# A gated mix of a Fourier layer and a SwiGLU layer: one row's product moved into a matrix, and comparisons moved in a hand-written queue

## The chip, the cores and the metric

The kernel runs on one core of one Trainium2 chip. Its engines are TensorE (matmul; PE in the profile, PEld its weight loads), VectorE (DVE), ScalarE (ACT), GpSimd (POOL) and SyncE (SP, which here only issues transfers). Matrix products land in PSUM, eight banks of 2 KB per partition; everything else is in the 128-partition SBUF. The metric is the device time of one execution in microseconds.

## The reference

For x of 2048 x 512 in float32 the result is g * a + (1 - g) * b:

```python
g = sigmoid((x * gate_w).sum(-1, keepdims=True))
# a: real part of a DFT over both axes, by the matrices handed in
a = dft_seq_re @ (x @ dft_hid_re.T) - dft_seq_im @ (x @ dft_hid_im.T)
# b: SwiGLU, hidden width 1376
b = (silu(x @ w1) * (x @ w3)) @ w2
```

## The kernel before, in words

Every float32 product is done as three fp32r products of a high and a low part (`mm3`: high-high, high-low, low-high). So each operand is split: `high` is a copy by ScalarE, `low` a subtraction by VectorE. TensorE runs the whole time, in these stages:

1. **Start** (C): the first product of gate/up, while x and the first weights are still arriving. Eleven warm-up matmuls (`wps`) go ahead of it. x's first quarter matrix `B11` is one load of 512 KB by SP, behind the first quarter of the weights `ws0`.
2. **Gate/up**, items 1 to 21: `gate_up(n)` makes one tile of `h = silu(gate) * up` by a Strassen-like scheme of seven half-size products, in banks X, Y and Z. `ITEMS` lists (chunk of the hidden width, half of the rows). In each item the products come in a fixed order: X, Z, the first product of item n+3, X, Z, the second product of item n+3, X. VectorE adds them up (`u4`, line 353; `u2`, lines 361 and 362; the last product, line 377). `h` goes to memory (`store_h`, issued by POOL), and so do the split second weights `wb`.
3. **H**: `h @ w2`, 22 steps of 24 matmuls (11 chunks, twice: once for each half of the rows), each into eight banks in the order `HB`. Each step loads a tile of `h` four steps ahead and splits it two steps ahead (`load_h`, `high_h`, `low_h`; `load_w2`, `high_w2`, `low_w2`). For steps 0 and 1 the splits are in the last item of gate/up, at its `mid` place, that is ahead of that item's lines 361 and 362 on VectorE. At the end of each half ScalarE and VectorE evict the banks, scaled by 1 - g (`nb`).
4. **O1, O2, E2**: the DFT over the rows, from parts of x that were added up by symmetry beforehand (`XF`) times folded DFT matrices (`MV`). Results are split into `Z`. Single rows that the folding leaves over are multiplied as products with one contracted row (`edge_p`, `er_p`).
5. **Y**: the DFT over the columns, ten units. A unit has an even part and an odd part in one pair of PSUM banks. In the even part the row of column 128 is a product of its own with one contracted row (`dx_p`), three matmuls between the two others. VectorE then does `r = Y * g + nb` in four operations (two for the last four units, which have half the rows), and SP stores `r`.

The fast way is right only if the DFT matrices have the symmetries of a DFT. So the kernel also **compares**: for each of the folded matrices O2, O1a, O1b and E2 (16 tiles of 512 KB each) it loads 15 tiles, subtracts the first from each or adds it (`differ`, VectorE, lines 699 to 705), and sums absolute values (`add_up`, ScalarE, line 710). Seven smaller tiles (`dh`) and one of single values go the same way. `verdict` then turns the sums into a flag, `verdict_end` counts it by a matmul, and if anything deviates a general path runs at the end (`tc.If`); with these inputs it doesn't.

These comparisons and the work on x (`make_pair`, `odd_part`, `spread`, `high_x`, `low_x`; in places POOL adds single rows, from `lone` on) are **tasks in a queue** that is filled in at build time, in program order: O2's comparisons, the pair sums of x, the `dh` comparisons, the forms of x, then O1a, O1b and E2. At fixed places of gate/up, H, O1, O2 and Y a call `work(engine, us)` takes the first tasks of that engine that are ready until the budget `us` is spent: a task is taken while the budget is at least its cost less `over`. A task is ready if its load was issued `LAG` calls ago (2 in gate/up, 4 in H) and the task before it has been taken. After each call `load_ahead` issues the loads of the next tasks, as long as there is a place in `F4` (SBUF tiles of 4 KB per partition, shared with the loads of `h` and `w2`), a token (`RATE` of them per call), and fewer than `AHEAD` open tasks. `LIMIT` says how far into the queue gate/up may reach: `n_spare` up to item 11, `n_gate` after it. Until item 11 has ended, `F4` has four places; the gate/up budgets for VectorE are 2.4 us in items 9 to 12 and 4.2 us after that. SP works its loads off in program order, and each load waits until its place has been read for the last time.

Of the kernel before, what the change touches and what calls it, by code (L numbers as in the profile page):

```python
# [30 lines left out]
def fnet_swiglu_gate_kernel(  # L31
# [60 lines left out]
    HELD = {}  # L92
# [13 lines left out]
    def free(*tiles):  # L106
        for t in tiles:
            _, places, at = HELD.pop(id(t))
            places.append(at)
# [56 lines left out]
    def load_xo(g, k):  # L166
# [4 lines left out]
        nc.sync.dma_start(ST[g, k], xt[g, XRAW.index(k)])  # L171
# [20 lines left out]
    def load_w(w, lo=0, hi=4):  # L192
        if lo == 0:
            WS[w] = f4_a.tile([P, 4, 256], F32, tag=f"f4_{4 + w % (LOOK + 1)}", name=f"ws{w}")
        nc.sync.dma_start(WS[w][:, lo:hi].rearrange("p a n -> p (a n)"),
                          w13[SETS[w], :, lo * 256 : hi * 256])
# [186 lines left out]
    load_w(0, 0, 1)  # L383
    load_xo(0, "B11")
# [171 lines left out]
    COLD, LAND, TOKENS, RATE = [], [4], [1.0], [0.9]  # L556
# [11 lines left out]
    def load_ahead(n):  # L568
        thaw()
        for i in ORDER:  # L570
# [3 lines left out]
            if sum(k not in ISSUED for k in LOADED) >= n or len(F4) < need + temps + HELD_BACK[0] + RES[0]:  # L574
# [9 lines left out]
    def work(eng, us, most=9, lag=None, over=0.3):  # L584
# [5 lines left out]
        for i in ORDER[:LIMIT[0]]:  # L590
# [5 lines left out]
            if i not in LOADED or NOW[0] - LOADED[i] < lag:  # L596
# [11 lines left out]
    AHEAD = [26]  # L608
# [62 lines left out]
    def high_x(form):  # L671
        XF[form] = [take(F4, [P, 1024], F32R, f"xf{h}_{form}") for h in range(2)]
# [122 lines left out]

    def make_d():
        def highs():
# [3 lines left out]
            nc.scalar.activation(DT[:, 0, 258:516], d[:, 258:516], AF.Copy, scale=-1.0)  # L801

        def lows():
# [3 lines left out]
            nc.vector.tensor_sub(DT[:, 1, 258:516], DT[:, 0, 516:].bitcast(F32), d[:, 258:516])  # L807
            free(DH.pop(1))
# [52 lines left out]
    def high_edges():  # L861
        high(edge_p[:1, 0], edge[:1])
        high(er_p[:1, 0], rowm[:1, :258])
        high(dx_p[:1, 0], rowm[:1, 258:388])
        high(lone_p[:, 0], lone_a)

    def low_edges():
        low(edge_p[:1, 0], edge_p[:1, 1], edge[:1])
        low(er_p[:1, 0], er_p[:1, 1], rowm[:1, :258])
        low(dx_p[:1, 0], dx_p[:1, 1], rowm[:1, 258:388])  # L870
# [8 lines left out]
    def lone():  # L879
# [4 lines left out]
        r0, r1 = ROWS  # L884
        nc.sync.dma_start(r0[:1], edges[:, :1024])
# [29 lines left out]
        g.memset(edge[:1, 257:258], 0.0)  # L915
# [9 lines left out]
    n_spare = 17  # L925
# [19 lines left out]
    do(early, SPARE[0], nc.vector.memset, tail, 0.0)  # L945
    for n in range(SPARE[0], NI):
        do(early, n, work, "D", 2.4 if n < SPARE[1] else 4.2 if n < NI - 3 else 3.2 if n < NI - 1 else 1.0)
# [7 lines left out]
    HB = (2, 3, 4, 5, 7, 6, 0, 1)  # L955
# [541 lines left out]
```

## Time and profile before

| | |
|---|---|
| runs | 369.67, 369.93, 370.22 us; median 369.93 |
| profiled execution | 370.23 us, of which the span from first to last instruction is 368.4 us |
| granted TensorE clock, mean | 0.995 |
| TensorE, VectorE, ScalarE busy | 357.5, 313.6, 234.9 us |
| moved by transfers | 102.79 MB, mean 279 GB/s |
| stages by the chain of waits: start, gate/up, H, O1 to E2, Y | from 5.6, 16.7, 206.9, 322.8, 338.3 us |

In a row of the timeline the first number is the start in us from the span's start, the second the duration of the merged instructions (`x12` merges twelve), then engine, line, operation and output<-inputs with shapes; a bracket at the end gives the idle time before and what ended it. In a row of a table by stretch, each engine's busy time and number of instructions follow the stretch's length, in the order TensorE, its weight loads, VectorE, ScalarE, POOL; then granted clock, transfer share and GB/s.

### The profile page before, as it was taken

How to read it: one execution, taken by the hardware profiler on the slowest of the kernel's cores; microseconds unless marked ns; L12 is line 12 of the kernel's file. 1: busy time of each engine (PE TensorE's matmuls, PEld its weight loads, DVE VectorE, ACT ScalarE, POOL GpSimd, SP SyncE). 2: the span in 40 equal slices, each digit the busy share in tenths (PEclk: the TensorE clock that was granted, in tenths of full speed). 3: DMA queues.
4: the chain of work that ended last, by engine and by line, in shares of the span. 5: the costliest groups of instructions: out<-in, count | busy, mean ns of one | idle time of the engine just before them, and what ended most of it. 6: DMA issues, size and time to landing. Idle time of an engine off the chain costs nothing.

```text
span 368.4 us, 5140 instructions
## 1 busy us (share of the span) xinstructions
PE 357.5 (97%) x1750; PEld 309.8 (84%) x1750; DVE 313.6 (85%) x433; ACT 234.9 (64%) x394; POOL 56.3 (15%) x95
## 2 busy tenths in 40 slices
PE   9999999999999999999999799999999999999982
PEld 5888888888888888888888688888888888898871
DVE  4999989999678897887878899889999799848991
ACT  5875766656666786774433665585589899784810
POOL 0001222111111111111110593700110020000000
PEclk9999999999999999999999999999999999999998
DMA  7549866666327889999998299775599999970584
GB/s 287 225 173 333 341 233 243 247 240 252 109 75 241 274 290 390 386 391 330 411 404 245 100 311 408 266 284 181 179 342 413 409 408 409 410 286 0 177 282 175
DMA packets 31922, 102.79 MB, mean 279 GB/s; under 512 B 5650, under 2 KB 5907, under 8 KB 29844
## 3 DMA queue, kind: packets, MB, share of 16 engines
q1 hardware_dynamic: 27060, 81.96, 61.1%
q0 software_dynamic: 4832, 20.46, 14.3%
q8 instruction: 15, 0.25, 0.3%
q14 instruction: 15, 0.12, 0.1%
HBM read 77.76 MB, written 24.65 MB: 278 GB/s over the span
## 4 chain that ended last, share of the span: by engine, by line
PE 84%; DVE 10%; ACT 3%; issue 1%; DMA 0%; SPq 0%; DVEq 0%; ACTq 0%
PE H L126 29%; PE X L126 28%; PE Z L126 14%; PE Y L126 7%; PE C L126 3%; DVE r L1237 3%; DVE t L705 2%; PE wps L388 1%; ACT nb L1098 1%; DVE z_O L115 1%; DVE ht L115 1%; DVE w2t L115 1%; PE Y L1210 1%; ACT z_O L112 1%; ACT t L710 1%
## 5 line engine op out<-in xcount | busy, mean ns | idle before, releaser
L126 PE MATMUL H<-w2t,ht 128*128 128x512 f32 (+1 forms) x528 | 114.5, 379 | 1.8 <-DVE h L361 1.8
L126 PEld LDWEIGHTS H<-w2t,ht 128*128 128x128 f32 (+1 forms) x528 | 99.6, 189 | 16.5 <-DVE h L361 2.2
L126 PE MATMUL X<-xo,wb 128*128 128x512 f32 x378 | 88.6, 379 | 0.0
L126 PEld LDWEIGHTS X<-xo,wb 128*128 128x128 f32 x378 | 71.4, 189 | 10.1
L710 ACT ACTIVATE t<-t 128x1024 f32<-128x1024 f32 (+1 forms) x68 | 67.7, 997 | 13.6 <-DVE t L699 5.9
L302 POOL DMA_DIRECT2D hs<-h x36 | 19.5, 543 | 99.3 <-DVE h L362 70.5
L699 DVE TENSOR_TENSOR t<-t,rep 128x1024 f32<-128x1024 f32 x28 | 32.9, 1218 | 1.8 <-DMA t<-wt 1.8
L373 ACT ACTIVATE h<-X 128x512 f32<-128x512 f32 x21 | 12.5, 595 | 28.7 <-PE X L126 28.3
L126 PE MATMUL X<-xo,wa 128*128 128x512 f32 x126 | 30.6, 379 | 0.0
L126 PE MATMUL Y<-xo,wa 128*128 128x512 f32 x126 | 30.6, 379 | 0.0
L126 PE MATMUL Z<-xo,wb 128*128 128x512 f32 x126 | 30.6, 379 | 0.0
L126 PE MATMUL Z<-xo,wa 128*128 128x512 f32 x126 | 30.6, 379 | 0.0
L701 DVE TENSOR_TENSOR t<-t,rep 128x1024 f32<-128x1024 f32 x24 | 28.2, 1218 | 0.0
L126 PEld LDWEIGHTS X<-xo,wa 128*128 128x128 f32 x126 | 23.8, 189 | 3.4
L126 PEld LDWEIGHTS Y<-xo,wa 128*128 128x128 f32 x126 | 23.8, 189 | 3.4
L126 PEld LDWEIGHTS Z<-xo,wb 128*128 128x128 f32 x126 | 23.8, 189 | 3.4
L126 PEld LDWEIGHTS Z<-xo,wa 128*128 128x128 f32 x126 | 23.8, 189 | 3.4
L112 ACT ACTIVATE ht<-hr 128x1024 fp32r<-128x1024 f32 x19 | 20.0, 1052 | 8.3 <-issue 6.3
L353 DVE TENSOR_TENSOR u<-u,X 128x512 f32<-128x512 f32 x21 | 14.4, 687 | 12.7 <-PE X L126 9.0
L115 DVE TENSOR_TENSOR ht<-hr,ht 128x1024 fp32r<-128x1024 f32 x19 | 23.1, 1216 | 0.9 <-ACT ht L112 0.9
L115 DVE TENSOR_TENSOR wa<-ws,wa 128x768 fp32r<-128x768 f32 (+1 forms) x22 | 19.3, 880 | 5.1 <-ACT wa L112 4.9
L112 ACT ACTIVATE wa<-ws 128x768 fp32r<-128x768 f32 (+2 forms) x21 | 16.9, 807 | 9.8 <-DMA ws<-w 6.2
(201 smaller groups left out, 499.2 us busy)
## 6 DMA issues: line engine op xcount, KB each, us to landing
t<-wt SPq DMA_DIRECT2D x60, 512.0 KB, 9.3
hr<-hs SPq DMA_DIRECT2D x19, 512.0 KB, 7.7
hs<-h POOLq DMA_DIRECT2D x36, 256.0 KB, 4.2
wbsp<-wb POOLq DMA_DIRECT2D x8, 1024.0 KB, 4.3
wb<-wbsp SPq DMA_DIRECT2D x8, 1024.0 KB, 9.6
ws<-w SPq DMA_DIRECT2D x11, 512.0 KB, 4.9
xs_B<-xt SPq DMA_DIRECT2D x8, 512.0 KB, 5.3
xr<-xw SPq DMA_DIRECT2D x8, 512.0 KB, 9.6
```

What stands on the lines that cost most here:

```text
L112: nc.scalar.activation(hi, src, AF.Copy)
L115: nc.vector.tensor_sub(lo, src, hi.bitcast(F32))
L126: nc.tensor.matmul(ps.rearrange("p (n a) -> p n a", a=2), u, turns(v)[:, some], **kw)
L302: nc.gpsimd.dma_start(hs[c][:, b * TB : (b + 1) * TB], h)
L353: nc.vector.tensor_add(u4, u4, x)
L373: nc.scalar.activation(g1, x, AF.Silu)
L388: nc.tensor.matmul(wps, warm[:, :P], warm, start=True, stop=True)
L699: nc.vector.tensor_sub(t, t, r)
L701: nc.vector.tensor_add(t, t, r)
L705: nc.vector.tensor_tensor(tv, tv, r[:, None, 512 * im : 512 * im + 512].to_broadcast([P, 2, 512]), op=ALU.add if im else ALU.subtract)
L710: nc.scalar.activation(t[:, :n], t[:, :n], AF.Abs, accum_out=acc[:, i : i + 1])
L1237: nc.vector.scalar_tensor_tensor(rv[:, :, h], src, g_pos[:, k : k + 1], nv[:, :, h], op0=ALU.mult, op1=ALU.add)
```

## The change

- `dx`, the row of column 128, is written (high and low part) into row 0 of the first 130 columns of both imaginary parts in `DT`. That row was zero, as sin(0) is. The product with the imaginary part then contains it, and the separate product with `dx_p` goes.
- `edge` and `rowm` are zeroed by POOL on all partitions, and `edge_p` and `er_p` are split and multiplied with all 128 partitions instead of one.
- From the end of item 4 to the end of item 15 the two places `ZO` (free in that time) are lent to `F4`. `n_spare` goes from 17 to 32, which is all of O2's comparisons; VectorE's budgets in items 9 to 12 are 1.2, 4.6, 3.5 and 3.5 us; ScalarE gets a call in items 5 to 8.
- Queue: `AHEAD` 14, counting only tasks with loads; at most four places held back; `RATE` 0.75 in the second half of H; larger budgets and a lag of 2 in the last step of H; in Y smaller budgets, and the rest of the queue and `verdict` at unit 4 instead of 7.
- `low_h(1)` and `low_w2(1)` move to the end of the last item; bank 7 is last in `HB`; `next_two` takes the PSUM pairs in another order.
- x's first load is in two pieces; the first weights' load is issued by ScalarE's queue, and so are the stores of the last two units.

```diff
+            if places is not F4 or at not in GONE:
+                places.append(at)
...
-    def load_xo(g, k):
+    def load_xo(g, k, pieces=1):
...
+        n = 1024 // pieces
+        for i in range(pieces):
+            nc.sync.dma_start(ST[g, k][:, i * n : i * n + n], xt[g, XRAW.index(k), :, i * n : i * n + n])
...
-    load_w(0, 0, 1)
-    load_xo(0, "B11")
+    load_w(0, 0, 1, nc.scalar)
+    load_xo(0, "B11", 2)
...
-            if sum(k not in ISSUED for k in LOADED) >= n or len(F4) < need + temps + HELD_BACK[0] + RES[0]:
+            if sum(k not in ISSUED and QUEUE[k][5] > 0 for k in LOADED) >= n or len(F4) < need + temps + min(HELD_BACK[0], HOLD[0]) + RES[0]:
...
-            if i not in LOADED or NOW[0] - LOADED[i] < lag:
+            if i not in LOADED or NOW[0] - LOADED[i] < lag or temps and len(F4) < temps + RES[0]:
...
-    AHEAD = [26]
+    AHEAD = [14]
...
     def high_x(form):
+        F4.sort(key=lambda at: at[0] is f4_a)
...
+    def first_d(h):
+        return DT[:1, h, 258:].rearrange("p (b m) -> p b m", b=2)[:, :, :130]
+    def dx_row():
+        return rowm[:1, None, 258:388].to_broadcast([1, 2, 130])
...
+            high(first_d(0), dx_row())            # in make_d, highs
+            low(first_d(0), first_d(1), dx_row()) # in make_d, lows
...
-        high(edge_p[:1, 0], edge[:1])
-        high(er_p[:1, 0], rowm[:1, :258])
-        high(dx_p[:1, 0], rowm[:1, 258:388])
+        high(edge_p[:, 0], edge)
+        high(er_p[:, 0], rowm[:, :258])
...
+        g.memset(rowm, 0.0)
+        g.memset(edge, 0.0)
...
-        g.memset(edge[:1, 257:258], 0.0)
...
-    n_spare = 17
+    n_spare = 32
...
+    do(at_end, SPARE[0] - 5, lend)
+    do(at_end, SPARE[1] + 2, give_back)
+    for n in range(SPARE[0] - 4, SPARE[0]):
+        do(second, n, work, "A", 1.3)
...
-        do(early, n, work, "D", 2.4 if n < SPARE[1] else 4.2 if n < NI - 3 else 3.2 if n < NI - 1 else 1.0)
+        do(early, n, work, "D", (1.2, 4.6, 3.5, 3.5)[n - SPARE[0]] if n < SPARE[1] else
+           4.2 if n < NI - 3 else 3.2 if n < NI - 1 else 1.0)
...
-    HB = (2, 3, 4, 5, 7, 6, 0, 1)
+    HB = (2, 3, 4, 5, 6, 0, 1, 7)
...
-        do(mid, NI - 1, low_h, m)
-        do(mid, NI - 1, low_w2, m)
+        do(at_end if m else mid, NI - 1, low_h, m)
+        do(at_end if m else mid, NI - 1, low_w2, m)
...
+        RATE[0] = 0.65 if begins else 0.75
+        late = 2 if last and not begins else None
...
-                d_left = work("D", (0.6 if last else 1.7 if begins else 2.0) + d_left, over=0.6)
+                d_left = work("D", ((0.6 if begins else 3.4) if last else 1.7 if begins else 2.0) + d_left,
+                              lag=late, over=0.6)     # the second call of a step: 4.4 instead of 3.4
...
-        chain_two(even, [(zs(0, za), same_d(0, 130)), (zs(1, zb, 1), same_d(0, 130, dx_p[:1])),
-                         (zs(1, zb), both_d(0, 130))])
+        chain_two(even, [(zs(0, za), same_d(0, 130)), (zs(1, zb), both_d(0, 130))])
...
+        by = nc.sync if u < 8 else nc.scalar
+        by.dma_start(out[FIRST[u] : FIRST[u] + n].rearrange("k p n -> p k n"),
...
-        if u < 7:
+        if u < 4:
             work("A", 3.6)
-            work("D", 2.4)
-        if u == 7:
+            work("D", 1.3)
+        if u == 4:
             work_until(set(range(n_late)))
             verdict()
```

More of the change, by code (lines that the diff above doesn't have):

```diff
@@ L554, in task @@
         return ORDER[-1]
-    COLD, LAND, TOKENS, RATE = [], [4], [1.0], [0.9]
+    COLD, LAND, TOKENS, RATE, HOLD = [], [4], [1.0], [0.9], [4]
     def free_later(*tiles):
@@ L1039, in fnet_swiglu_gate_kernel @@
     DT, lone_p = own("dt", [P, 2, 774], F32R), own("lone_p", [P, 2, 8], F32R)
-    edge_p, er_p, dx_p = (own(k, [P, 2, n], F32R) for k, n in (("edge_p", 258), ("er_p", 258), ("dx_p", 130)))
+    edge_p, er_p = (own(k, [P, 2, 258], F32R) for k in ("edge_p", "er_p"))
     edge, rowm, few, spc = (own(k, [P, n]) for k, n in (("edge", 258), ("rowm", 392), ("few", 4), ("spc", 32)))
@@ L1083, in fnet_swiglu_gate_kernel @@
             if j == 6:
-                d_left = min(work("D", (0.6 if last else 1.7 if begins else 2.0) + d_left, over=0.6), 1.0)
+                d_left = work("D", ((0.6 if begins else 4.4) if last else 1.7 if begins else 2.0) + d_left,
+                              lag=late, over=0.6)
+                d_left = min(d_left, 1.0)
                 if m % 2 and not last:
@@ L1132, in edge_of @@
     def edge_of(lo, hi):
-        return [edge_p[:1, h, lo:hi] for h in range(2)]
-    er_of, dx_of = ([t[:1, h] for h in range(2)] for t in (er_p, dx_p))
+        return [edge_p[:, h, lo:hi] for h in range(2)]
+    er_of = [er_p[:, h] for h in range(2)]
     def forms(to_a, to_b, fs, pars, p):
```

38 lines of the change are left out of this document (21 added, 17 removed).

## The prediction

> **What bounds the kernel now.** I read the page first: its first parts say which engine is full, and when.
>
> ```profile
> span 368.4 us, 5140 instructions
> PE 357.5 (97%) x1750; PEld 309.8 (84%) x1750; DVE 313.6 (85%) x433; ACT 234.9 (64%) x394; POOL 56.3 (15%) x95
> PEclk9999999999999999999999999999999999999998
> GB/s 287 225 173 333 341 233 243 247 240 252 109 75 241 274 290 390 386 391 330 411 404 245 100 311 408 266 284 181 179 342 413 409 408 409 410 286 0 177 282 175
> ```
>
> TensorE is full and at full clock, so a gain must take matmuls away or close one of its few gaps. The slices of GB/s show a ceiling near 410 late in gate/up and in the second half of the H product, and idle transfer time in slices 10 and 11. Busy PE hides waits between matmuls, so the timeline comes second. First the last stage: ten units Y, each 15 matmuls, four or two evictions `r` on VectorE, and comparisons `t` between them.
>
> ```profile
> 338.29 0.60 PE L1210 MATMUL Y<-dt,z_O 128*128 128x260 f32 x3
> ...
> 341.76 1.65 DVE L1237 SCALAR_TENSOR_TENSOR r<-Y,tail,nb 128x256 f32<-128x256 f32 x4
> 342.96 0.60 PE L1210 MATMUL Y<-dx_p,z_O 1*128 1x260 f32 x3
> 343.32 2.35 DVE L705 TENSOR_TENSOR t<-t,rep 128x1024 f32<-128x1024 f32 x2
> 343.49 1.61 PE L1210 MATMUL Y<-dt,z_O 128*128 128x260 f32 x12
> 345.03 0.60 PE L1210 MATMUL Y<-dx_p,z_O 1*128 1x260 f32 x3
> 345.59 1.65 DVE L1237 SCALAR_TENSOR_TENSOR r<-Y,tail,nb 128x256 f32<-128x256 f32 x4
> ...
> 359.05 0.19 PE L545 MATMUL count<-const-float32-1.0,tail 128*1 128x1 f32 x2 [0.74 <-DVE tail L542]
> 361.54 0.88 DVE L1237 SCALAR_TENSOR_TENSOR r<-Y,tail,nbr 128x256 f32<-128x256 f32 x2 [1.80 <-PE Y L1210]
> 362.44 0.33 SPq L1239 DMA_DIRECT2D out<-r  x1
> ```
>
> From one dx group to the next, 342.96 to 345.03, is a unit: 2.07 us. Of it the three one-row dx matmuls take 0.53 (342.96 to 343.49) and the other twelve 1.54. Ten units would be 20.7, but Y runs from 338.29 to 361.54, 23.25: the missing 2.55 is TensorE behind VectorE, which spends 3.8 a unit (345.59 less 341.76), and behind the verdict. So here VectorE's comparisons are the bound and the dx group is second.
>
> The one long gap elsewhere is at the first H step (timeline, and last a row of the chain that ended last):
>
> ```profile
> 206.50 1.59 POOL L890 TENSOR_TENSOR row<-row 1x512 f32<-1x512 f32 x1 [16.60 <-DVE ht L115]
> 206.86 2.80 PE L126 MATMUL H<-w2t,ht 128*128 128x512 f32 x12
> 206.88 2.30 DVE L115 TENSOR_TENSOR ht<-h,ht 128x1024 fp32r<-128x1024 f32 x1
> 210.77 0.68 DVE L361 TENSOR_TENSOR h<-h,Z 128x512 f32<-128x512 f32 x1
> 211.50 3.72 PE L126 MATMUL H<-w2t,ht 128*128 128x512 f32 x16 [1.84 <-DVE h L361]
> ...
> 211.50 107.13 PE H L126 x495
> ```
>
> After four blocks TensorE waits 1.84 for L361: the fifth uses bank 7, whose last gate/up result VectorE reads only after `low_h(1)` and `low_w2(1)`. `low_h(1)` is slow (2.30, where a comparison of its size takes 1.22 at 107.44 below) while POOL's row sums run. A matmul of H takes 107.13 / 495 = 0.216, a step of 24 of them 5.19.
>
> **The change part by part**, against the profiled execution: 370.23 us, of which 368.4 is span; the median of the runs, 369.93, is 0.3 lower.
>
> *dx into DT, comparisons out of Y.* Thirty dx matmuls go: 10 x 0.53 = 5.3. What remains costs 10 x 1.54 = 15.4, if VectorE keeps up. I stepped the queue's rules through both versions (a budget is spent while it is at least cost less `over`; a comparison is ready two calls, in H four, after its load; a load needs a free place and a token). Before, the E2 comparisons 7 to 15, nine of them, fall after H; that is the row L699 at 330.1 and all eight L705. Afterwards the last six are issued in the last H step and none in O1 or Y. VectorE then has 1.65 a unit in the six double units and 0.88 in the four single ones: 13.4 in all and the verdict's two short operations, never more than a unit or so behind TensorE, which has four PSUM pairs. With the verdict at u = 4 the `count` matmul finds its input ready and costs about 0.3. Y: 15.4 + 0.3 for 23.25, **gain 7.6**. The bounds are 6.1, if the 0.14 a group by which the three are dearer than three of the other twelve (1.54 / 4 = 0.385) stays with their neighbours, and 7.6.
>
> The Trainium skill, "TensorE: Matmul & The Clock Gate", section "Why this matters for your kernels", has a matmul of 32 contracted rows take as long as one of 128. By that the dx group would cost what three full matmuls cost, 0.385, and Y would gain 6.1; this trace disagrees, at 0.53.
>
> *Full-partition edges.* In the E product:
>
> ```profile
> 333.76 0.60 PE L126 MATMUL E<-er_p,edge_p 1*128 1x258 f32 x3
> 334.28 1.61 PE L126 MATMUL E<-mov_E,xf_E 128*128 128x258 f32 x12
> ```
>
> Three one-row matmuls take 0.52, twelve full ones 1.54, so three full ones 0.385. Two such groups give 0.27; a third, with one column, I leave at 0. **Gain 0.3**, between 0 (the price is the switch's and stays) and 0.65 (the third costs as much too much, and leaves idle time). ScalarE's and VectorE's splits have the same columns, one copy and one subtraction move from `make_edges` to `make_d`; nothing. The two memsets stand on POOL ahead of the row sums, where POOL has idled 16.6 us; nothing if they run then, at most their length, under 1 us, in a chain discussed below.
>
> *`low_h(1)`, `low_w2(1)` last; bank 7 last.* L361 now follows `low_w2(0)`, at about 206.9, and bank 7 is wanted at 206.86 + 21 x 0.216 = 211.4. The 1.84 goes. Next late is `w2t(1)` for the second H step at 212.05. Undisturbed it is done near 210.5; at the slowed durations above near 213. Row sums should start earlier than 206.5, as their places are free sooner (`t` of the hidden matrix, not the first `h`). **Gain 1.8**, between 0.8 and 1.8.
>
> *Two more places.* Items 9 to 14 had 0, 1, 2, 2, 3, 2 comparisons and get 1, 4, 2, 3, 2, 3. What VectorE had free in items 9 to 18, and in item 10 alone:
>
> ```profile
> 97.00:187.70 90.70, 90.70 (x422) 79.43 (x421) 71.96 (x95) 56.45 (x100) 12.25 (x23) 1.00 0.84 305
> 106.10:115.10 9.00, 9.00 (x43) 7.90 (x42) 7.30 (x14) 6.72 (x13) 0.72 (x2) 1.00 0.76 239
> ```
>
> The third busy column is VectorE, the fourth ScalarE; the last two are the share and GB/s of the transfers. VectorE idles 18.7 us in the ten items. The sum fits, the order does not quite: in item 10 three comparisons more (1.14 each: two end in 2.35, one in 1.22) stand ahead of `u4`:
>
> ```profile
> 107.44 1.22 DVE L699 TENSOR_TENSOR t<-t,rep 128x1024 f32<-128x1024 f32 x1
> 108.58 0.42 DVE L217 TENSOR_TENSOR wu<-ws 128x256 f32<-128x256 f32 x1
> ...
> 111.30 0.69 DVE L353 TENSOR_TENSOR u<-u,X 128x512 f32<-128x512 f32 x1 [1.17 <-PE X L126]
> 113.62 0.59 PE L126 MATMUL X<-xo,wb 128*128 128x512 f32 x2
> ```
>
> 107.44 + 4 x 1.14 + four `wu` 1.5 = 113.5, L353 ends at 114.15 and X at 113.62 waits for it: **loss 0.5**, with what follows between 0 and 2. Item 12's extra one ends before its X. There is a second way to lose: on SP a `t` load that waits for its place holds the next `ws` load behind it, and `wa` and then X wait for that.
>
> ```profile
> 90.59 18.25 SPq L694 DMA_DIRECT2D t<-wt  x2
> 113.96 0.85 ACT L112 ACTIVATE wa<-ws 128x768 fp32r<-128x768 f32 x1 [1.94 <-DMA ws<-w]
> ```
>
> That happens now without reaching TensorE. Afterwards items 11 and 12 have it: the third load of the item before waits for a sum at that item's end (about 117.8), `ws` lands some 4 us later, and `wa` is wanted for 126.7. Covered by 2 us or more in my count. The extra ScalarE sums fall in the 2.3 us that ScalarE has free there. Items 17 to 21 then hold the small `dh` comparisons in place of pair sums: no more VectorE time.
>
> *The rest of the queue* (loads by need, AHEAD 14, RATE 0.75, late budgets): ten comparisons more in H, six pieces of form work fewer, about 6 us of VectorE against what it idles there, and seven loads more. H is where the second bound is:
>
> ```profile
> 264.70:311.50 46.80, 46.80 (x218) 40.99 (x217) 44.28 (x42) 43.32 (x73) 5.39 (x8) 1.00 0.98 379
> hr<-hs SPq DMA_DIRECT2D x19, 512.0 KB, 7.7
> ```
>
> Transfers are nearly full there and run past H: 286 GB/s in the 36th slice of 9.2 us are 2.6 MB. By my count five loads (2.6 MB) more are done by the middle of H, so the last comparison's data should come about when H ends. An `h` load is issued four steps (20.8 us) ahead and lands in 7.7, so TensorE is covered even when a load takes twice that. Taken at **0**, bounds 0 and -4.
>
> *Start.* Two halves of x, and the first `w` from ScalarE's queue, so that x is first on SP:
>
> ```profile
> 0.76 4.85 PE wps L388 x11
> 5.62 11.04 PE C L126 x48
> 5.02 0.94 ACT L112 ACTIVATE xo<-xs_B 128x256 fp32r<-128x256 f32 x2 [1.48 <-DMA xs_B<-xt]
> ```
>
> x can come about 1 us sooner, but the warm-up matmuls hold TensorE until about 5.1 of the 5.5, and the 48 matmuls (48 x 0.216 = 10.4 of 11.04) meet B21's load, which stays where it was. **Gain 0.2**, between -0.1 and 0.8. ScalarE's issue lies ahead of its first work.
>
> The Trainium skill, "DMA: Bandwidth & Descriptors", section "Issuing engines are not separate DMA queues", says that a second issuing engine saves only the time to issue. By that the last stores would gain nothing, as here, and the start at most one issue, 0.33 us in the row of 362.44.
>
> *Last stores by ScalarE.* From the last issue (362.44) to 368.4 are 6.0 us: landing, each engine's read of the flag, the end. ScalarE takes SP's place in the same order: 0, bounds -0.3 and 0.5.
>
> **Sum**: 7.6 + 0.3 + 1.8 - 0.5 + 0 + 0.2 + 0 = 9.4; 370.23 - 9.4 = **360.8 us** (360.5 against the median). I predict 360.8.
>
> **The rivals.**
> *Data too late* (for: the 410 GB/s ceiling; against: five loads' lead).
>
> ```profile
> 326.56 0.69 DVE L1156 TENSOR_TENSOR s<-e,O 128x512 f32<-128x512 f32 x1 [5.76 <-ACT e L1155]
> 334.78 1.23 DVE L115 TENSOR_TENSOR z_O<-s,z_O 128x1024 fp32r<-128x1024 f32 x1 [1.12 <-ACT z_O L112]
> ```
>
> If the lead is lost, the last comparison's data lands where the transfers ended before, 322.4 + 2.6 MB / 410 GB/s = 328.8, and holds VectorE to 330. From the first `s` to the end of z_O took 9.45 (326.56 to 336.01) with two comparisons, 2.3, among it; ScalarE's sums, now late too, put about 1.4 back: z_O at 338.6 on the old clock, where Y could start at 336.5 (338.29 less 0.2, 1.8 and 0.3, plus 0.5). That is 2.1 us, 362.9.
>
> *POOL's row sums are late for the form work.*
>
> ```profile
> 222.73 0.19 POOL L921 TENSOR_TENSOR lone_b<-two 128x2 f32<-128x2 f32 x1
> 226.28 0.72 POOL L829 COPY xo_O1a<-row 1x256 f32<-1x256 f32 x1 [3.35 <-DVE xo_O1a L652]
> 235.92 1.06 ACT L112 ACTIVATE xf_O1a<-xm_O1a 128x1024 fp32r<-128x1024 f32 x1 [4.36 <-POOL xm_O1a L668]
> ```
>
> That chain is 16.4 us long (206.50 to 222.9). The form work moves up by two H steps (10.4 us), so `spread` wants L829 near 218: started as late as before, POOL holds VectorE 5 us, and behind it stand `low_h(4)` for the step at 227.6. I find 2.5 us lost there at most, with a late `w2t(1)` 3.5: 364.3. Against it: the row loads no longer wait.
>
> *The other side*: comparisons uncovered in gate/up. They stand ahead of L353, whose slack is one 1.3 us product and 1.2 of idling. Slower is reached when nine of the 15 in items 9 to 14 stall X by their whole 1.14 (9.4 / 1.14 = 8.2); with ten it is 11.4 for 9.4, 372.2. Against it: the 18.7 us that VectorE idles in items 9 to 18.
>
> *A dx group is worth no more than three full matmuls*: its extra 0.14 belongs to the stream around it and stays, and the edges gain nothing; 0.3 and 1.5 less, 362.6. Against it: the rows above, where only the one-row groups are slow, in Y and in E alike. So it would go by the rule of the Trainium skill, "TensorE: Matmul & The Clock Gate", cited above.
>
> **How the numbers follow.** Chances: forecast 0.60 (359.4 to 362.2, from its smaller bounds), data late 0.12, POOL late 0.13, equal price 0.04, better at the start, in item 10 and the end together 0.06 (to 358.8), the other side 0.05. The range 358.9 to 364.8 takes in all but the far ends of POOL's case and the other side. A change of 0.2%, 0.7 us, is about what the measurement tells from none. Faster 0.94, same 0.02, slower 0.04.
>
> **What would show it.** Right: Y with 12 matmuls a unit, 1.54 apart, and no idle before `count`; no L705 after H; H's first 24 matmuls without a gap; a wait of X on L353 of about 0.5 near 113.6. Wrong: gaps in H (`ht` late behind POOL or behind `hr`), a VectorE wait on `t` loads after H, units at 1.6 or more because the `r` or the `nbr` loads set them.

## The result, and the profile after

| | before | after |
|---|---|---|
| median of four runs, us | 369.94 (369.67 to 370.22) | 365.47 (364.77 to 366.16) |
| ratio, 95% interval | | 0.9879 (0.9857 to 0.9901) |
| profiled execution / its span, us | 370.23 / 368.4 | 364.77 / 363.0 |

The kernel is 4.5 us faster, 5.4 in the profiled pair; the forecast was 9.4. Two runs, one of e14 below (412.9 us, at a granted clock of 0.85) and one of the kernel before in that round (1332.7 us), stand in no median and no ratio. The page of the changed kernel:

```profile
span 363.0 us, 5082 instructions
PE 349.7 (96%) x1720; PEld 303.7 (84%) x1720; DVE 313.2 (86%) x433; ACT 235.2 (65%) x394; POOL 64.0 (18%) x96
```

TensorE has 7.8 us less work, so 2.4 of that came back as idle time. In the last stage, Y, the timeline shows where (start, length, engine, line, what; in brackets the wait before it):

```profile
338.93 8.22 PE L1243 MATMUL Y<-dt,z_O 128*128 128x260 f32 x72
346.99 4.19 PE L1243 MATMUL Y<-dt,z_E 128*128 128x260 f32 x36
...
351.61 1.58 PE L1243 MATMUL Y<-dt,z_E 128*128 128x260 f32 x12 [0.30 <-DVE r L1269]
...
352.17 0.88 DVE L1269 SCALAR_TENSOR_TENSOR r<-Y,tail,nbr 128x256 f32<-128x256 f32 x2 [0.71 <-DMA nbr<-nbsp]
354.12 0.88 DVE L1269 SCALAR_TENSOR_TENSOR r<-Y,tail,nbr 128x256 f32<-128x256 f32 x2 [1.08 <-DMA nbr<-nbsp]
...
355.98 0.88 DVE L1269 SCALAR_TENSOR_TENSOR r<-Y,tail,nbr 128x256 f32<-128x256 f32 x2 [0.93 <-issue]
...
347.93 0.76 SPq L1229 DMA_DIRECT2D nbr<-nbsp  x1
348.78 0.90 SPq L1272 DMA_DIRECT2D out<-r  x1
349.77 0.87 SPq L1229 DMA_DIRECT2D nbr<-nbsp  x1
```

TensorE runs through six double units in 8.06 us (338.93 to 346.99: 72 matmuls, 0.112 each, 1.34 a unit) and is done with Y at 353.2, 14.3 us after it began, where it took 23.2 before. But VectorE's last three `r` each wait, and the last one starts 2.8 us behind TensorE's end: the loads of `nbr` stand on SP between the stores `out`, each of which waits for its `r`, and the last is issued at 349.77. For the last `r` the profile names no releaser ("issue"); its load had been issued 6.2 us earlier, and the six loads of `nbr` take 5.2 to 6.1 us from issue to landing. So Y ends at 356.86 (before: 362.42).

In gate/up, the queue of SP, then ScalarE, then TensorE:

```profile
110.53 9.02 SPq L698 DMA_DIRECT2D t<-wt  x3
119.61 0.42 SPq L198 DMA_DIRECT2D ws<-w  x1
...
125.62 0.84 ACT L113 ACTIVATE wa<-ws 128x768 fp32r<-128x768 f32 x1 [2.90 <-DMA ws<-w]
...
128.13 1.04 ACT L714 ACTIVATE t<-t 128x1024 f32<-128x1024 f32 x1
...
129.28 0.60 ACT L343 ACTIVATE h<-X 128x512 f32<-128x512 f32 x1
...
114.42 2.86 PE L127 MATMUL X<-xo,wb 128*128 128x512 f32 x12 [0.41 <-DVE u L356]
129.93 1.56 PE L127 MATMUL X<-xo,wb 128*128 128x512 f32 x6 [0.75 <-ACT h L343]
```

Three loads of `t` hold SP for 9.02 us, the load of `ws` behind them leaves at 119.61, ScalarE stands 2.90 us at `wa`, and what follows in its order is late: a sum of a comparison (128.13) and behind it the copy `h<-X` (129.28), for which X at 129.93 waits. With the pace of the products (1.30 a group of six) taken off, TensorE loses 0.56 at 114.42, 1.01 at 129.93, 0.37 at 153.97 behind `wb`, and 0.1 in each of six places.

At the first step of H:

```profile
209.44 1.23 DVE L116 TENSOR_TENSOR w2t<-w2r,w2t 128x512 fp32r<-128x512 f32 x1
...
209.76 0.38 PE L127 MATMUL H<-w2t,ht 128*128 128x512 f32 x1
210.73 5.45 PE L127 MATMUL H<-w2t,ht 128*128 128x512 f32 x24 [0.59 <-DVE w2t L116]
```

One gap of 0.76 (210.73 less 209.76 less 0.216) stands here, where the kernel before had one of 2.05 (211.50 less 206.86 less 12 x 0.216). All stages, from the timelines of the profiled pair:

| us | before | after | gain | forecast |
|---|---|---|---|---|
| start, to the first product X | 16.49 | 16.73 | -0.24 | 0.2 |
| gate/up, to H | 190.37 | 193.03 | -2.66 | -0.5 |
| H and O, to E | 126.13 | 124.83 | 1.30 | 1.8 |
| E | 5.30 | 4.34 | 0.96 | 0.3 |
| Y, to the end of the last `r` | 24.13 | 17.93 | 6.20 | 7.6 |
| behind it | 5.98 | 6.14 | -0.16 | 0 |

### The profile page after: what moved, and what is told of

Same layout as the page of the kernel before. It is cut to its first block, busy times and chain, and to the rows that moved or that the text cites. A ratio compares the mean times of both kernels' runs of the same rounds, so it can differ in the third digit from the quotient of the medians.

```text
span 363.0 us, 5082 instructions
## 1 busy us (share of the span) xinstructions
PE 349.7 (96%) x1720; PEld 303.7 (84%) x1720; DVE 313.2 (86%) x433; ACT 235.2 (65%) x394; POOL 64.0 (18%) x96
## 4 chain that ended last, share of the span: by engine, by line
```

## Experiments

Each kernel is the changed kernel with the edit shown, unless told otherwise. "Expected" is as it was written before the run. Times are medians; "ratio" is to the kernel before, with its 95% interval. First the changed kernel again:

> The changed kernel without any edit, timed beside its variants so that each is read against it on one chip. The first runs gave 364.77 to 366.16 us. Expected: 365.4 us, 364.6 to 366.2; a wider spread would mean that differences under 1 us between variants can be told only from their traces.

Measured: 365.3 us (364.45 to 366.19), ratio 0.9871 (0.9855 to 0.9888). Variants of this kernel spread by 1 to 2 us where the kernel before spreads by 1, so traces decide small differences.

### Y: what the row in the matrix was worth

dx alone, in the kernel before:

```
-  chain_two(even, [(zs(0, za), same_d(0, 130)), (zs(1, zb, 1), same_d(0, 130, dx_p[:1])), (zs(1, zb), both_d(0, 130))])
+  chain_two(even, [(zs(0, za), same_d(0, 130)), (zs(1, zb), both_d(0, 130))])
```

> Edit: the kernel before with dx alone: its row goes into DT, and the one-row products with dx_p in Y go (30 matmuls); edges, queue, start and stores as before. Theory 1 (in the kernel before, DVE has 19.93 us of work in the 23.50 us of Y, six comparisons of 1.22 among it, so that without them TensorE would wait for r): Y's last r comes 1.5 to 2.5 us earlier, 367.5 to 368.5 us; the rest of what Y gained came from the comparisons that the queue took out of it. Rival 2 (TensorE alone paces Y): the 30 matmuls and their slowed neighbours are worth 5.3 to 7.6 us at once, 362.4 to 364.6 us.

Measured: 370.05 us, ratio 1.0002 (0.9993 to 1.0011): nothing. The timeline of Y in this kernel:

```profile
338.67 6.98 PE L1216 MATMUL Y<-dt,z_O 128*128 128x260 f32 x60
347.77 2.15 PE L1216 MATMUL Y<-dt,z_O 128*128 128x260 f32 x12 [2.13 <-DVE r L1242]
351.61 6.16 PE L1216 MATMUL Y<-dt,z_E 128*128 128x260 f32 x36 [1.68 <-DVE r L1242]
```

TensorE takes 60 matmuls at 0.114 and then stands behind VectorE, which is busy for 21.46 of the 23.5 us. Behind the first stand its granted clock falls to 0.50 (from 349.8 to 354), and matmuls follow each other in 0.21 us; that cost nothing here, since VectorE set the pace. Theory 1 named the bound and still gave it 2 us too much. The reverse, the queue with dx's one-row matmuls back:

```
+  ..., (zs(1, zb, 1), same_d(0, 130, dx_p[:1])), ...      # and dx_p split in make_edges, not in make_d
```

> Edit: the changed kernel with dx_p and its 30 one-row matmuls in Y back; queue, edges, start and stores as changed. Theory 1 (Y had two bounds next to each other, TensorE with the one-row matmuls and DVE with the comparisons; dx alone gave 0.1 us because DVE stayed full): without comparisons but with the 30 matmuls TensorE takes 20 to 22 us for Y instead of 14.25, no r waits for nbr, the last r ends near 361 us, and the time is 369 to 371 us: the queue alone is worth as little as dx alone. Rival 2 (the queue was the whole gain, the matmuls lay beside DVE's r): 365 to 366.5 us, with Y's end set by nbr as in the changed kernel.

Measured: 368.29 us, ratio 0.9955 (0.9941 to 0.9969).

```profile
341.30 0.60 PE L1244 MATMUL Y<-dx_p,z_O 1*128 1x260 f32 x3
341.83 1.61 PE L1244 MATMUL Y<-dt,z_O 128*128 128x260 f32 x12
...
338.80:360.90 22.10, 21.15 (x154) 18.32 (x152) 14.93 (x38) 2.85 (x6) 0.00 (x0) 1.00 0.69 251
```

The last row is the whole of Y, busy time of TensorE first: now TensorE is full (21.15 of 22.10), VectorE has 14.93, and no `r` waits for `nbr`. So Y had two bounds side by side: up to the end of its last `r` it takes 24.13 us before, 23.41 with dx alone, 22.07 with the queue alone and 17.93 with both. In the whole time dx alone gave 0.1 us, the queue (with all else) 1.7, both together 4.5. Theory 1 holds; only its time was about 1 us high, since the stretch behind the last `r` was 4.9 us here.

The edges, back on one partition:

```
-  return [edge_p[:, h, lo:hi] for h in range(2)]
+  return [edge_p[:1, h, lo:hi] for h in range(2)]         # and so er_p, and their splits
```

> Edit: the changed kernel with edge_p and er_p split and multiplied on one partition again, as in the kernel before. Theory 1 (a matmul on one row slows the full ones beside it): E takes 5.3 to 5.5 us instead of 4.34, its matmuls of 258 columns 0.128 us each instead of 0.112, and the end moves by 0.3 to 1.0 us, less than E, if the loads of nbr set Y's end. Rival 2 (E got shorter because the comparisons beside it went): E stays at 4.3 to 4.5 us, nothing moves.

Measured: 365.91 us, ratio 0.9883 (0.9867 to 0.9898). In the timeline, E with one-row edges, and below it E of the changed kernel:

```profile
336.24 0.60 PE L127 MATMUL E<-er_p,edge_p 1*128 1x258 f32 x3
336.77 1.61 PE L127 MATMUL E<-mov_E,xf_E 128*128 128x258 f32 x12
338.31 0.60 PE L127 MATMUL E<-er_p,edge_p 1*128 1x258 f32 x3
```

```profile
335.26 0.50 PE L127 MATMUL E<-er_p,edge_p 128*128 128x258 f32 x3
335.59 1.50 PE L127 MATMUL E<-mov_E,xf_E 128*128 128x258 f32 x12
336.93 0.50 PE L127 MATMUL E<-er_p,edge_p 128*128 128x258 f32 x3
```

The twelve full matmuls take 1.54 us (336.77 to 338.31) between one-row groups and 1.34 (335.59 to 336.93) without. E is 5.30 against 4.34 us, as theory 1 has it. But its mechanism, that the full ones are slowed, is not what the trace shows. The starts of single matmuls in e6 follow each other in 0.205 us into a one-row group, 0.215 behind its first matmul, 0.199 back into the full ones and 0.214 behind the first of those; every other step is 0.110 to 0.113, among one-row matmuls as among full ones. So each pair of changes costs 0.385 us (the four steps less 4 x 0.112), and the group and its neighbours share it. Two such groups and the last one, which has a single column and only two long steps (0.203 and 0.198), make 0.95 of the 0.96. The end moved by 0.6 us, hidden in part behind `nbr`.

The loads of `nbr` on a queue of their own:

```
-            nc.sync.dma_start(NB[u].rearrange("p (k n) -> p k n", k=2)[:, :n],
+            nc.gpsimd.dma_start(NB[u].rearrange("p (k n) -> p k n", k=2)[:, :n],
```

> Edit: the loads of nbr in Y are issued by POOL, on whose queue no store of a result stands ahead of them; same places, same order. Theory 1 (the last loads came late only because SP issued each behind the store of the unit before, which waits for that unit's r): nbr8 and nbr9 land before their unit's matmuls end, no r waits for a DMA, the last r ends about 1.1 us (its four steps of 0.48, half of them behind the unit's last matmul at 353.0) to 1.9 us after TensorE, at 354.1 to 354.9 instead of 356.86: 2.0 to 2.8 us less in all, 363 us. Rival 2 (the DMA engines are full at the end: 347 GB/s in the slice ahead of the last): the loads land earlier and the stores that share the engines land later, and the end moves by less than 0.5 us. Rival 3 (the place, not the queue, holds the loads): nothing moves.

Measured: 362.51 us, ratio 0.9807 (0.9780 to 0.9834), 2.8 us less than the changed kernel beside it. The end in its timeline:

```profile
349.29 4.00 DVE L1269 SCALAR_TENSOR_TENSOR r<-Y,tail,nbr 128x256 f32<-128x256 f32 x10
...
353.48 0.88 DVE L1269 SCALAR_TENSOR_TENSOR r<-Y,tail,nbr 128x256 f32<-128x256 f32 x2
...
351.87 1.58 PE L1243 MATMUL Y<-dt,z_E 128*128 128x260 f32 x12 [0.31 <-DVE r L1269]
```

No `r` waits for a DMA, and the last begins as TensorE ends (353.45). The queue held the loads, not the places or the DMA engines: theory 1.

### Gate/up: what held TensorE

`ws` and `wb` issued by ScalarE, so that SP may stand at the loads of `t`:

```
-            load_w(wa, 0, 3 if back(wa) else 4)
+            load_w(wa, 0, 3 if back(wa) else 4, nc.scalar if n > 8 else nc.sync)   # and load_wb
```

> Edit: in gate/up from item 9 on, the loads of ws and wb are issued by ScalarE at the start of the item instead of by SP; the loads of t stay on SP, and what DVE and ScalarE compute stays in its order. Theory 1 (a load of t that waits for its place holds the next ws and wb behind it on SP, and through the wait of wa's high half ScalarE's copy of u is late): the gap of 1.01 us at X of item 12 (129.93, wait on L343) and the 0.37 us at 153.97 (wait on wb) go, the 0.56 us at 114.42 (wait on DVE's L356) stays: 1.0 to 1.4 us less, about 364.2 us. Rival 2 (two more comparisons an item simply fill ScalarE and DVE): the gaps stay, within 0.3 us of the changed kernel.

Measured: 374.44 us, ratio 1.0125 (1.0110 to 1.0141): 9 us slower than the changed kernel. In its timeline:

```profile
114.70 2.86 PE L127 MATMUL X<-xo,wb 128*128 128x512 f32 x12 [0.40 <-DVE u L356]
...
129.18 1.46 PE L127 MATMUL X<-xo,wb 128*128 128x512 f32 x6
...
140.93 1.56 PE L127 MATMUL X<-xo,wb 128*128 128x512 f32 x6 [2.51 <-ACT h L343]
...
122.90 0.84 ACT L113 ACTIVATE wa<-ws 128x768 fp32r<-128x768 f32 x1
...
127.27 1.04 ACT L714 ACTIVATE t<-t 128x1024 f32<-128x1024 f32 x1
...
119.51 11.91 SPq L698 DMA_DIRECT2D t<-wt  x8
131.47 15.71 SPq L631 DMA_DIRECT2D xr<-xw  x8
```

Both theories fail as a time. The gap at item 12 is gone with the same work on VectorE and ScalarE: `ws` is in time (`wa` at 122.90 without a wait), the sum stands in ScalarE's line as before (127.27), and X at 129.18 does not wait. The gap behind VectorE stays (114.70). Both are as theory 1 has them. But with no `ws` between them SP runs through eight loads of `t` and eight of `xr` in a row, and transfers then stand at 408 GB/s (140 to 150 us). ScalarE, which now issues `ws` in its own order, comes to that at 139.82 and to the copy for X at 140.28; this `ws` is waited for until 148.07. TensorE loses 2.7 us before 140.93 and 3.4 before 154.16, and behind the latter its granted clock is 0.50 until 160, which costs 2.9 more. The edit changes who issues `ws` and what holds SP back at once, so that the standing on SP had also kept the loads apart is argued, not shown.

Smaller budgets instead:

```
-        do(early, n, work, "D", (1.2, 4.6, 3.5, 3.5)[n - SPARE[0]] if n < SPARE[1] else
+        do(early, n, work, "D", (1.2, 2.4, 2.4, 2.4)[n - SPARE[0]] if n < SPARE[1] else
```

> Edit: the changed kernel with budgets of 1.2, 2.4, 2.4, 2.4 us instead of 1.2, 4.6, 3.5, 3.5 in gate/up's items 9 to 12; places are lent out at once as in the changed kernel. 22 of the comparisons' instructions stand in gate/up instead of 24 (20 in e12). Theory 1 (loads of t standing at their places hold ws on SP): the 0.56 us behind DVE at 114.4 shrinks, as item 10 has two comparisons less, but waits of X on ScalarE's copy of u2 remain, 0.7 us or more in all, and H starts at 209.0 to 209.8: 364.5 to 365.3 us. Rival 2 (the amount of work in items 10 to 13 alone): the waits go as in e12, H starts by 208 us, 362 to 363 us.

Measured: 362.52 us, ratio 0.9785 (0.9769 to 0.9801).

```profile
111.02 1.36 SPq L698 DMA_DIRECT2D t<-wt  x2
112.44 0.42 SPq L198 DMA_DIRECT2D ws<-w  x1
```

Rival 2 gave the time: H starts at 207.64, and gate/up takes 190.42 us from the first X, as before the change. It does not refute theory 1, though: with fewer loads in line none of their sets holds SP for more than 2.61 us, and `ws` leaves at 112.44 instead of 119.61. The two causes fell together. A third edit, of when a place is lent out again:

```
         nc.scalar.activation(t[:, :n], t[:, :n], AF.Abs, accum_out=acc[:, i : i + 1])
-        free(t)
+        free(t) if LIMIT[0] == n_late else free_later(t)     # LAND = 2 in gate/up
```

> Edit: in gate/up a place that a t leaves is lent out again two turns of the queue later, so that the load that takes it finds it free and SP does not stand at it; 20 comparisons in gate/up instead of 24, 51 in H, none in O and Y. Theory 1 (t loads that wait for their place hold the next ws on SP; unlike in e2, nothing lets the loads run ahead of their pace): SP issues ws within 1 us of its item's start, the waits of X on ScalarE's copy of u2 (0.75 us at 129.9, in one run also at 140) go, the wait on DVE at 114.4 stays: H starts 1.0 to 1.9 us earlier than at 209.8 to 210.2, and the time is 363.8 to 364.4 us. Rival 2: the same waits stand with SP free, so that ScalarE itself is late: 365 to 365.5 us.

Measured: 361.92 us, ratio 0.9789 (0.9776 to 0.9801), better than either theory's range.

```profile
103.18 0.43 SPq L198 DMA_DIRECT2D ws<-w  x1
110.57 7.88 SPq L698 DMA_DIRECT2D t<-wt  x3
118.55 0.39 SPq L198 DMA_DIRECT2D ws<-w  x1
...
120.57 0.83 ACT L113 ACTIVATE wa<-ws 128x768 fp32r<-128x768 f32 x1
...
131.22 0.83 ACT L113 ACTIVATE wa<-ws 128x768 fp32r<-128x768 f32 x1
...
16.70:207.40 190.70, 190.70 (x884) 166.49 (x883) 168.33 (x245) 120.01 (x204) 36.01 (x71) 1.00 0.77 282
```

TensorE is busy for all 190.70 us of gate/up (the first busy column), though one set of loads still holds SP for 7.88 us. The `ws` behind that set is not the one that was late before: loads and copies pair in order, so the one that leaves at 118.55 is copied at 131.22, without a wait, and the one that left at 119.61 in the changed kernel leaves here at 103.18 and is copied at 120.57. So e12, e16 and e2 all have that `ws` in time, and in none X waits at item 12. e12 and e16 also have fewer sums there; e2 has the same ones, so it is the late `ws` that cost the 1.01 us. Without the sum at 128.13 the copy behind it would have come 1.15 us earlier (129.28 less 128.13), so by this estimate the late `ws` needed that sum to reach TensorE; no run has the one without the other.

Gate/up's queue as before, all else as changed:

```
-    n_spare = 32
+    n_spare = 17            # no places lent, budget 2.4
```

> Edit: in gate/up the queue is filled as in the kernel before (15 comparisons instead of 24, budget 2.4 us an item, no two places lent); all else as changed. The nine comparisons then stand in H (52 instead of 47) and O (4 instead of 0); none in Y. Theory 1 (the nine comparisons and their loads cost TensorE 2.66 us in gate/up, and H and O have room for them, as O had in the kernel before, where its four took nothing): H starts 2.3 to 2.7 us earlier, H and O keep their lengths within 0.3 us, 363.0 us. Rival 2 (the places were needed: in H DVE or the loads come late): what gate/up gains comes back in H, O or Y, 365 to 367 us.

Measured: 364.89 us, ratio 0.9869 (0.9850 to 0.9889). H starts 1.8 to 2.2 us earlier, at 207.95, and H keeps its length; Y took 17.0 us on TensorE and its last `r` ended at 357.83, so what was gained in front was lost at the end: nearer to rival 2. Six comparisons stand behind H there, none in the changed kernel, and TensorE waits 0.59 us for `z_E` at 340.75 and more than 1 us behind `r` at the verdict. Taking the comparisons out of O and Y was needed.

### The first step of H

```
-    row_u, row_v = lone()
...
+                if m == 0: row_u, row_v = lone()      # behind the first three matmuls of H
```

> Edit: the loads of the edge rows and POOL's sums over them are issued behind H's first eight-bank step's first three matmuls instead of ahead of H. Theory 1 (DVE's low of w2t took 1.23 us instead of 0.69 because POOL's sums ran beside it, and the second third of H's matmuls waited for it): the gap of 0.97 us between 209.76 and 210.73 shrinks by 0.4 to 0.7 us, the time with it, provided that what waits for the sums (the row put into the first form) still comes in time. Rival 2 (the gap is set by ScalarE's high of w2t, and the low would end as late): nothing moves. Rival 3 (the sums end too late for the forms): H gets a wait of 1 us or more.

Measured: 366.04 us, ratio 0.9886 (0.9867 to 0.9904). The edit didn't do what it says: nothing makes POOL wait for the place in the program, and its first sum ran from 204.75 as soon as the row had landed. So POOL was held by data:

```
+        g.tensor_copy(few[:1, 0:1], WT[1][:1, 512:513].bitcast(F32))
```

> Edit: the changed kernel with POOL's sums over the edge rows held until DVE's low of the second w2t (in e4 they weren't held: POOL started at 204.75 all the same). Theory 1 (POOL's sums beside DVE make DVE's comparisons with dh take 1.37 and 1.63 us in place of 0.29 and 0.55, or w2t's low 1.22 in place of 0.69, whichever they meet): both at their short times, the gap at H's second matmul falls from 0.9 to 1.0 us to 0.2 to 0.4, and the time by 0.5 to 0.8. Rival 2 (the sums now end too late for the forms): H gets a wait. Rival 3: nothing moves, the sums were not the cause.

Measured: 369.11 us (367.32 to 372.14), ratio 0.9982 (0.9958 to 1.0006). Its timeline and its table of waits:

```profile
204.74 0.29 DVE L779 TENSOR_TENSOR t<-t,dh 128x130 f32<-128x130 f32 x1
204.94 0.56 DVE L781 TENSOR_TENSOR t<-t,dh 128x386 f32<-128x386 f32 x1
...
209.42 0.69 DVE L116 TENSOR_TENSOR w2t<-w2r,w2t 128x512 fp32r<-128x512 f32 x1
...
209.77 4.54 PE L127 MATMUL H<-w2t,ht 128*128 128x512 f32 x19
```

```profile
PE H L127 <- ACT nb L1132: 1.7, 1, 1.7
PE H L127 <- DVE w2t L116: 1.2, 1, 1.2
```

Theory 1 has the mechanism: `w2t`'s low takes 0.69 instead of 1.23, and H begins without a gap; a later low, at 215.49, now runs beside the sums and takes 1.78. Rival 2 has the time: the sums end near 227 us, VectorE waits 2.65 us for them there, and TensorE 1.2 at 232.32 behind it. H pays 1.7 more at 270.60, behind ScalarE's evictions; that this too comes from the late sums was not followed back.

### The start, the stores, and all together

```
-    load_w(0, 0, 1, nc.scalar)
+    load_w(0, 0, 1)
```

> Edit: the very first load (ws, first of four parts) is issued by SP again, ahead of x, and x still comes in two pieces. Theory 1 (the load by ScalarE landed at about 4.8 us where SP's had landed before 3.1, and the first matmul of C waits for it): C starts at 5.4 to 5.6 instead of 6.04, the first product of gate/up at 16.3 to 16.5 instead of 16.73: 0.2 to 0.4 us less. Rival 2 (x in two pieces is what costs): C stays at 6.0. Rival 3: C starts earlier and a later load of w holds the chain, nothing is left at 16.73.

Measured: 365.6 us, ratio 0.9881 (0.9862 to 0.9900). C starts at 5.05 instead of 6.04, but X at 16.96: rival 3. In its trace the next loads of x, now behind `ws` on SP, are late in turn: ScalarE's copy at 8.32 waits 0.90 us for one.

Kernels that put edits together:

> Edit: the changed kernel with nbr loaded by POOL (e1), gate/up's queue as before (e7), and POOL's sums over the edge rows held until DVE's low of the second w2t (a one-element copy on POOL that reads it). Theory 1 (three separate costs): H starts near 207.9 us as in e7, Y's last r ends 0.9 us after TensorE's last matmul as in e1, no wait on w2t at H's start, so that H starts to O in 115 us or less: Y starts at 337.0 us, TensorE ends near 351.3, last r 352.2, span 358.6, time 360.4 us (359.6 to 361.2). Rival 2 (in e7 O and H carry nine comparisons more, and Y took 16.97 us there instead of 14.25; if that was DVE and not nbr, it stays): 362 to 363 us.

Measured: 362.22 us, ratio 0.9803 (0.9782 to 0.9825). H starts at 207.24, but Y takes 17.6 us on TensorE with `nbr` early: rival 2. As in e7, TensorE waits for `z_E` (0.83 us) behind comparisons that stand behind H.

> Edit: e12 and e1 together: places of t lent out two turns later in gate/up, nbr loaded by POOL. Theory 1 (two separate costs, both of SP's queue): H starts as in e12 (207.4), TensorE ends Y near 350.3, and the two waits of r on nbr and on its issue (1.6 and 1.3 us in e12) go: 2.9 us less than e12's 361.92, 359.0 us (358.4 to 359.7). Rival 2 (the DMA engines, at 407 GB/s in e12 between 346 and 350 us, set the end when Y comes earlier): 360.5 to 361.9 us.

Measured: 361.24 us (359.38 to 363.32), ratio 0.9746 (0.9724 to 0.9769). The profiled run, the slowest of the six, lost 1.7 us before the first X and 2.3 in gate/up, mostly behind `wb` and `u`; its last `r` followed TensorE at once.

> Edit: e13 with places of t lent out one turn later instead of two; 22 of the comparisons' instructions in gate/up instead of 20. Theory 1 (a load stands as long as its place is in use: one turn, half an item, is often less than what a comparison and its sum need): a part of the waits comes back, 0.3 to 1.0 us: 359.3 to 360.0 us. Rival 2 (only loads that stand for several us matter): as e13, within 0.3 us.

Measured: 360.43 us, ratio 0.9744 (0.9722 to 0.9766): within the spread of e13, so that neither theory is refuted.

> Edit: e13, with the start (ws first by SP, x in one piece) and the last stores (by SP) as in the kernel before. Theory 1 (both changes of the start and the end cost what the trace shows): gate/up starts at 16.5 instead of 16.77 and the stretch from the last r to the end is 0.1 to 0.3 us shorter: 0.3 to 0.6 us less than e13, 358.5 us. Rival 2 (differences within the spread of runs, or SP's queue holds the last stores longer): within 0.2 us of e13.

Measured: 359.12 us (358.75 to 361.95), ratio 0.9705 (0.9685 to 0.9725), the lowest of all, but its X began at 16.90, not 16.5: the gain isn't the start's.

> Edit: the changed kernel with e16's budgets (1.2, 2.4, 2.4, 2.4) and nbr loaded by POOL (e1). Theory 1 (two costs, both found, nothing else of their size): e16's 362.52 less the waits of r on nbr and its issue (1.4 and 0.9 us in its trace): 360.2 us (359.5 to 360.8); with the prediction's 360.8 its two failed terms would then be told. Rival 2 (loads of nbr, early, meet other traffic, as wb's did in e13): 361 us or more.

Measured: 360.18 us (359.80 to 360.41), ratio 0.9732 (0.9719 to 0.9745): theory 1, as expected, and 5.1 us under the changed kernel. Gate/up, H and Y by busy time (TensorE first, then weight loads, VectorE, ScalarE):

```profile
16.70:207.50 190.80, 190.76 (x883) 166.35 (x882) 168.72 (x246) 119.55 (x205) 33.27 (x64) 1.00 0.77 281
207.50:322.70 115.20, 114.32 (x528) 99.91 (x529) 111.32 (x125) 89.13 (x147) 26.24 (x33) 1.00 0.89 340
...
337.00:352.30 15.30, 14.02 (x125) 13.63 (x122) 14.16 (x38) 3.89 (x8) 0.00 (x0) 1.00 0.64 237
```

What is left idle is 0.9 us in H, at its start, and 1.3 in Y, most of it beside the last `r`. It is faster than both kernels.

> Edit: e17 with the start (ws first by SP, x in one piece) and the last stores (by SP) as in the kernel before. Theory 1: gate/up starts near 16.5 instead of 16.75 to 17.2, and the stretch behind the last r is 6.0 instead of 6.1 to 6.3: 0.3 to 0.7 us less than e17, 359.7 us. Rival 2: within 0.2 us of e17.

Measured: 360.88 us, ratio 0.9753 (0.9739 to 0.9766), 0.7 more than e17. X began at 16.83, and H waited 1.6 us for `w2t` where e17 waited 0.86. The old start and stores bring nothing back.

## Why the prediction was wrong

The sign was right and the size was not: 360.8 was forecast, 365.5 measured, above the range (358.9 to 364.8). Two steps failed. The late `ws` was held to be "covered by 2 us or more" and cost 1.01 us, the largest part of a gate/up term that was 2.66 and not 0.5. And Y was to cost 15.4 us "if VectorE keeps up", "never more than a unit or so behind", where VectorE ended 3.7 us behind TensorE, because the loads of `nbr` had no price. By its steps:

- *dx into DT, comparisons out of Y* (7.6): 6.2, inside its bounds (6.1 to 7.6), but by luck, as two errors partly cancel. TensorE's part was larger than both bounds, 14.3 us for 23.2, since each unit lost the two changes to and from one-row matmuls as well: 0.73 us a unit (2.07 less 1.34), not 0.53. Against it stands the step that failed. VectorE's budget of 13.4 us was right (14.32 busy with E's last), but the loads that it waits for were not priced; the `nbr` loads stand among what would show the prediction wrong, with no time beside them. They took 2.8 us of TensorE's 9.0 back. e1 shows the queue as the cause.
- *Edges* (0.3): 0.96 in E. I had counted only the step of the groups themselves; the steps back into the full matmuls go too (e6). The rival by which the extra 0.14 "belongs to the stream around it and stays" is refuted. The rule cited from the Trainium skill, "TensorE: Matmul & The Clock Gate", section "Why this matters for your kernels", by which a matmul of 32 contracted rows takes as long as one of 128, is not contradicted by these groups: within one, matmuls of a single row follow each other in 0.112 us, as full ones do. The 0.53 that the prediction held against it has the changes in it.
- *`low_h(1)` and bank 7 last* (1.8): the old gap went. What is late next is not `w2t(1)`, as I wrote, but `w2t(0)`, slowed by POOL's sums, which start earlier as I had said. Cost 0.76; e10 shows the cause. The Trainium skill, "SBUF — State Buffer", section "Who interferes with whom", says that a VectorE instruction with two SBUF inputs contends with a GpSimd one that reads SBUF; this trace agrees (0.69 alone, 1.23 beside the sums).
- *Two more places* (-0.5, bounds 0 to -2): the wait at 114 came as written, 0.56 for 0.5. The second way to lose was described and then dismissed. The sum that frees the place was put 2 us too early (117.8; `ws` left at 119.61) and the landing 4 us too early (about 121.8; ScalarE had it at 125.6). Even so the cover to the product of `wa` held: that product did not wait. But ScalarE works in order, and its copies for the item's first bank stood behind `wa`'s high half: that is what X met. Together -2.66; e16 and e12 take all of it away, and e2 shows the late `ws` as the cause of its largest piece.
- *Rest of the queue* (0): right. H has no wait for data, and no comparison follows H. Neither "data too late" nor "POOL's row sums are late" happened; e10, which made the sums late, shows that the second was a real danger.
- *Start* (0.2): -0.24. The first `ws` landed 4.1 us after its issue by ScalarE, beside the two loads of x, where it took 2.4 by SP ahead of them, so C began later for all that x came in pieces. e3 shows that an earlier C isn't worth anything at X.
- *Last stores* (0): -0.16, within its bounds.

With the two failed terms repaired by two small edits (e17), the time is 360.2, close to the forecast, but in part by luck. Of its 9.8 us Y gives 9.0 (7.6 was forecast) and E 1.0 (0.3), H and O only 0.9 (1.8), and the start and the stretch behind the last `r` lose 0.6 where 0.2 was to be gained. That dx and the queue are worth little alone (0.1 and 1.7 us; e5, e9), the prediction had in part: it called VectorE the bound of Y and dx second, and summed them as one term.

## What to carry to other kernels

When an engine's work is cut, price the next things in line at the stage's end, loads included: find on which queue each is issued and what stands ahead of it there. A load that waits for its place holds every later load of its queue, and an engine that waits for one of those holds everything behind it in its own order, so follow a delay through to the work behind, not only to its own consumer. And before moving such a load to a free queue, ask whether the standing was also what kept the transfers apart. Last, price a few odd-shaped matmuls by what goes when they go, the steps around them included, and not by the time of their own row.

## What the runs showed of the hardware that was not expected

- Changing between matmuls that contract one row and full ones costs time at the change, not in the matmul: four steps of 0.20 to 0.215 us in place of 0.112 for each one-row group, 0.385 us in all, in E of the kernel before and of e6 alike; within the group a step is 0.112. Why, no run shows.
- Behind a stand of TensorE its granted clock fell to one half: in e2 to 0.50 from 154 to 160, behind one of 3.4 us, with 0.43 us for a matmul of 0.216; in e5 to 0.50 around 352, behind one of 2.3. In the changed kernel, where gate/up stood 1.01 us at most, it stayed at 1.00 there.
- The first load of 128 KB landed 4.1 us from its issue by ScalarE beside loads of x, and 2.4 us by SP ahead of them (e3). Whether the issuing engine or the company made the difference, no run separates.
- The place in the program did not hold POOL back: its sums began at 204.75 in e4 and at 204.82 in the changed kernel; a copy that reads the tile to wait for held it until 213.94 (e10).
- The Trainium skill, "DMA: Bandwidth & Descriptors", section "Issuing engines are not separate DMA queues", says that starting transfers from several engines saves only the time to start them. e1 differs in effect: the same loads from another queue ended the kernel 2.8 us earlier, since nothing stood ahead of them.
